# Setup of a fused attention and expert kernel: one activation table set, second-layer weights moved behind the first rows, one exp for both head parities of the last keys, one operation less in routing

## The chip, the cores and the metric

The kernel runs on one core of a Trainium2 chip. The metric is the time of one execution in microseconds (us) of device time. The engines are named as the profile names them: PE (matmuls; PEld is its weight load), DVE (vector), ACT (scalar, with function tables), POOL (general, here mostly the issuer of DMAs), SP (issuer of further DMAs). Each engine runs its own instructions in order and waits on the others by semaphores.

## The reference

Attention with a learned position bias (FIRE), then a mixture of eight experts in which every token has a given expert.

```python
# attention: batch 8, heads 8, seq 576, head_dim 64; hidden 32
scores = scale * q @ k^T
psi_rel = log1p(abs(i - j)); psi_i = log1p(max(i, 1))
x = (psi_rel / psi_i)[..., None]
bias = relu(x @ w1 + b1) @ w2            # one bias per (i, j, head), the same for all batches
attn = softmax(scores + bias)
x_rows = (attn @ v) as 4608 rows of 512  # batch and seq together, all heads side by side
# experts: 8 of them, 512 -> 1024 -> 512
out[rows of e] = relu(x_rows[rows of e] @ w1[e]) @ w2[e]
```

## The kernel before, in words

The program has three stages. **The bias stage** (the head of the program, up to about 56 us) computes exp(bias) once, for all heads, into fp16 tables that stay on chip: `biasM` for the keys 0 to 511, `biasR` for the last 64 keys, `biasL` and `biasRL` for the last 64 queries. **The attention stage** runs over eight batches; for each, 20 units of scores are made on PE, exponentiated on ACT (L585), multiplied by the tables on DVE (L596), and multiplied by v on PE (L609, L613). Its rows are scattered by POOL to DRAM (L673), sorted by expert. **The expert stage** (from about 226 us) reads them back transposed and runs the two matmuls of each expert on PE (L814, L790).

PE, DVE and ACT run their instructions in the order in which the program writes them (a manual schedule); POOL and SP are ordered by the framework's scheduler. The order around the change is as follows.

`_setup_constants` loads w1, b1 and w2 by three small DMAs on SP (L134, L136, L138), makes index ramps on POOL (L140 to L145), their logarithms on ACT (L158 to L165, L182, L183), and on DVE the slopes (L160 to L169), the negated b1 (`nb1`, L174) and `W2BIG` (L176, L178): a block-diagonal copy of w2, with four query rows times eight heads as its 32 columns. It is the second layer's weights. Then come, on DVE, the first operation of routing (L326) and three memsets of `_Attention.__init__` (L450, L452).

`_phase_bias` runs nine blocks `ib` of 64 queries (the ninth for the last 64). `hidden(ib)` makes 16 rows of hidden units, one per `k16`, each a tile of 128 (four queries times 32 units) by 576 keys: on ACT as a Relu with scale and bias (L220) for some `k16`, on DVE as multiply and max (L223) for the others. `outputs(ib)` takes the 16 rows through PE in three groups of keys: two groups of 2 x 128 keys (L240, 64 matmuls, 32 columns each) and the last 64 keys (L244, 16 matmuls with 64 stationary columns, into partitions 0 to 63 only). ACT exponentiates each group from PSUM: `biasM` in two operations (L256), and `biasR` in two operations of 64 partitions, one for the even and one for the odd heads (L253), each into its own half of the partitions. One raw part is copied by DVE (L260). The three groups share three PSUM buffers (`eb`). The program calls `hidden(ib + 1)` before `outputs(ib)`, so that the row work of a block stands ahead of the exponentials of the block before it. A row tile is used again two blocks later.

`_phase_route` is a generator: a chain of small DVE operations on 128x320 tables that gives each token its row in the sorted buffer; it is advanced by `next(route)` between the rows of the first blocks, and its rest (L352 to L408) runs on DVE at block 8, before the first attention units. Two of those operations are the overflow mask: `past = incl >= CAP` (L393) and `past = past * obase` (L395).

DMAs: POOL loads q, k and v of the first two batches and then weights, each issue waiting for an earlier one on its queue; SP copies the zeroed `vrag` tile to two others (L454) and fills the sorted buffer with zeros (L951), 9.25 MB.

Of the kernel before, what the change touches and what calls it, by code (L numbers as in the profile page):

```python
# [12 lines left out]
AO = mybir.AluOpType  # L13
AF = mybir.ActivationFunctionType
# [11 lines left out]
CAP = 640  # L26
# [11 lines left out]
NCOL = B * NT  # L38
# [36 lines left out]
def rap(t, off, dims, nparts=None):  # L75
    p0 = list(t.ap[0])
    if nparts is not None:
        p0[1] = nparts
    return bass.AP(tensor=t.tensor, offset=off, ap=[p0] + [list(d) for d in dims])
# [43 lines left out]
def _setup_constants(tc, G, w1, b1, w2):  # L123

    nc = tc.nc
    cst = G.cst
    w1col = cst.tile([P, 1], F32, tag="w1col", name="w1col")
    nc.sync.dma_start(out=w1col, in_=bass.AP(tensor=w1.tensor, offset=0, ap=[[0, 4], [1, 32], [1, 1]]))  # L134
    G.pb1 = cst.tile([P, 1], F32, tag="pb1", name="pb1")
    nc.sync.dma_start(out=G.pb1, in_=bass.AP(tensor=b1.tensor, offset=0, ap=[[0, 4], [1, 32], [1, 1]]))  # L136
    w2sb = cst.tile([HID, 8], F32, tag="w2sb", name="w2sb")
    nc.sync.dma_start(out=w2sb, in_=w2[:, :])  # L138
    li = G.tmp.tile([P, W4 + W1], I32, tag="li", name="li")
    nc.gpsimd.iota(li[:, 0:W4], base=-C4, channel_multiplier=0, pattern=[[1, W4]])  # L140
    si = G.tmp.tile([P, NGR], I32, tag="si", name="si")

    nc.gpsimd.iota(si[:, 0:128], base=0, channel_multiplier=0, pattern=[[1, 4], [16, 32]])
    nc.gpsimd.iota(si[:, 128:144], base=512, channel_multiplier=0, pattern=[[4, 16]])
    nc.gpsimd.iota(li[:, W4:], base=-(C1 + 512), channel_multiplier=0, pattern=[[1, W1]])  # L145

    gs = cst.tile([P, 5], F32, tag="gs", name="gs")
    nc.vector.memset(gs[:, 4:5], 1.0)
    for g in range(4):
        nc.vector.memset(gs[32 * g: 32 * g + 32, 0:1], float(g))  # L150
    for i, f in ((2, -4.0), (1, 4.0), (3, -1.0)):
        nc.vector.tensor_scalar(out=gs[:, i: i + 1], in0=gs[:, 0:1], scalar1=f, scalar2=None, op0=AO.mult)
    nc.vector.memset(G.zero[:, :, 0:DM], 0.0)
    lf = G.tmp.tile([P, W4 + W1], F32, tag="lf", name="lf")
    G.L4 = G.asb.tile([P, W4 + W1], F16, tag="L4", name="L4")
    G.slope = G.asb.tile([P, NGR], F32, tag="slope", name="slope")

    nc.scalar.activation(out=G.slope[:, 0:1], in_=gs[:, 4:5], func=AF.Ln, bias=1.0, scale=1.0)  # L158
    nc.scalar.activation(out=lf[:, 0:W4], in_=li[:, 0:W4], func=AF.Abs, bias=gs[:, 2:3], scale=1.0)
    nc.vector.tensor_scalar(out=G.slope[:, 0:128], in0=si[:, 0:128], scalar1=gs[:, 1:2], scalar2=1.0,  # L160
                            op0=AO.add, op1=AO.max)
    nc.vector.tensor_scalar(out=G.slope[:, 128:], in0=si[:, 128:], scalar1=gs[:, 0:1], scalar2=1.0,
                            op0=AO.add, op1=AO.max)
    nc.scalar.activation(out=G.slope, in_=G.slope, func=AF.Ln, bias=1.0, scale=1.0)
    nc.scalar.activation(out=G.L4[:, 0:W4], in_=lf[:, 0:W4], func=AF.Ln, bias=1.0, scale=1.0)  # L165

    def slopes(a, b):
        nc.vector.reciprocal(out=G.slope[:, a:b], in_=G.slope[:, a:b])
        nc.vector.tensor_scalar(out=G.slope[:, a:b], in0=G.slope[:, a:b], scalar1=w1col[:], scalar2=None,  # L169
                                op0=AO.mult)  # L170
    G.slopes = slopes
    slopes(0, 16)
    G.nb1 = cst.tile([P, 1], F32, tag="nb1", name="nb1")
    nc.vector.tensor_scalar(out=G.nb1, in0=G.pb1, scalar1=-1.0, scalar2=None, op0=AO.mult)  # L174
    G.W2BIG = G.asb.tile([P, 32], F16, tag="W2BIG", name="W2BIG")
    nc.vector.memset(G.W2BIG, 0.0)  # L176
    for g in range(4):
        nc.vector.tensor_scalar(  # L178
            out=G.W2BIG[32 * g: 32 * g + 32, 8 * g: 8 * g + 8],
            in0=w2sb, scalar1=8.0, scalar2=None, op0=AO.mult,  # L180
        )
    nc.scalar.activation(out=lf[:, W4:], in_=li[:, W4:], func=AF.Abs, bias=gs[:, 3:4], scale=1.0)  # L182
    nc.scalar.activation(out=G.L4[:, W4:], in_=lf[:, W4:], func=AF.Ln, bias=1.0, scale=1.0)  # L183
    G.idn = cst.tile([P, P], F16, tag="idn", name="idn")
    make_identity(nc, G.idn)


def _phase_bias(tc, G, route, at, fill):


    nc = tc.nc
    with tc.tile_pool(name="fps", bufs=1, space=bass.MemoryType.PSUM) as fps:
# [16 lines left out]
        def hidden(ib):  # L209
            hrl = []  # L210
            tiles = hidden_tiles(ib)
            for k16 in range(16):
                if ib < 8:
                    r, a = ib // 2, 16 * (ib % 2) + k16
                    m, c0 = 32 * r + a, C4 - (16 * a + r)
                else:
                    m, c0 = 128 + k16, W4 + C1 - 4 * k16
                hr = next(tiles)
                if k16 in ((2, 5, 8, 11, 14) if ib < 2 else (3, 8, 13)):
                    nc.scalar.activation(out=hr, in_=G.L4[:, c0: c0 + S], func=AF.Relu,  # L220
                                         bias=G.pb1[:], scale=G.slope[:, m: m + 1])
                else:
                    nc.vector.tensor_scalar(out=hr, in0=G.L4[:, c0: c0 + S],  # L223
                                            scalar1=G.slope[:, m: m + 1], scalar2=G.nb1[:],
                                            op0=AO.mult, op1=AO.max)
                hrl.append(hr)
                if (ib, k16) == (0, 7):
                    G.slopes(16, NGR)
                if (ib, k16) in ((1, 1), (1, 5), (1, 9), (2, 1), (2, 5)):
                    next(route)  # L230
            return hrl

        def outputs(ib, hrl):
            for jcs in ((0, 1), (2, 3), (4,)):
                eb = fps.tile([P, 2, 512], F32, tag="eb", name="eb", bufs=3)
                for k16 in range(16):
                    for lj, jc in enumerate(jcs):
                        hr = hrl[k16]
                        if jc < 4:
                            nc.tensor.matmul(out=eb[:, lj, 32 * k16: 32 * k16 + 32],  # L240
                                             lhsT=hr[:, jc: jc + 4 * 127 + 1: 4],
                                             rhs=G.W2BIG[:, 0:32], start=True, stop=True)
                        else:
                            nc.tensor.matmul(out=eb[0:64, lj, 32 * k16: 32 * k16 + 32],  # L244
                                             lhsT=hr[:, 512:576],
                                             rhs=G.W2BIG[:, 0:32], start=True, stop=True)
                ebv = eb.rearrange("p l (i h) -> p l h i", h=8)
                i0 = 64 * ib
                if jcs[0] == 4:
                    for h2 in range(2):  # L250
                        o = G.biasR[64 * h2: 64 * h2 + 64, :, i0: i0 + 64] if ib < 8 else \
                            G.biasRL[64 * h2: 64 * h2 + 64]
                        nc.scalar.activation(out=o, in_=ebv[0:64, 0, h2::2, :],  # L253
                                             func=AF.Exp, bias=0.0, scale=0.125)
                elif ib < 8:
                    nc.scalar.activation(out=G.biasM[:, jcs[0]: jcs[0] + 2, :, i0: i0 + 64], in_=ebv,  # L256
                                         func=AF.Exp, bias=0.0, scale=0.125)
# [3 lines left out]
                else:  # L261
                    for lj in range(2):
                        nc.scalar.activation(
                            out=G.biasL[:, jcs[0] // 2, lj, :, :, :].rearrange("p h q i -> p q h i"),
                            in_=ebv[:, lj, :, :].rearrange("p (q h) i -> p q h i", h=2),
                            func=AF.Exp, bias=0.0, scale=0.125)
# [36 lines left out]
def _phase_route(tc, G, dom2, x_dram):  # L303
# [7 lines left out]
    nc = tc.nc  # L311
# [10 lines left out]
    nc.gpsimd.memset(keep, 1.0)  # L322
    nc.gpsimd.memset(keep[:, :, 0:1], 0.0)
    nc.gpsimd.memset(keep[:, :, NCOL - NT: NCOL - NT + 1], 0.0)
    domf = pbuf.tile([P, NCOL], F32, tag="domf", name="domf")
    nc.vector.tensor_copy(out=domf, in_=dom2[:, :, :, 0].rearrange("p b t -> p (b t)"))  # L326
    yield
# [62 lines left out]
        nc.vector.tensor_tensor(out=v, in0=v, in1=rap(apref, i, [[2, 8], [0, c.stop - c.start]]), op=AO.add)  # L390
        yield
    past = pbuf.tile([P, 8, NCOL], F32, tag="past", name="past")
    nc.vector.tensor_scalar(out=past, in0=incl, scalar1=float(CAP), scalar2=None, op0=AO.is_ge)  # L393
    yield
    nc.vector.tensor_tensor(out=past, in0=past, in1=rap(obase, 0, [[1, 8], [0, NCOL]]), op=AO.mult)  # L395
    yield
    nc.vector.tensor_tensor(out=incl, in0=incl, in1=past, op=AO.add)
    yield
# [33 lines left out]
class _Attention:  # L432
# [10 lines left out]
    def __init__(self, tc, G, q, k, v, x_dram):  # L443
# [3 lines left out]
        nc, asb = self.nc, G.asb  # L447
        self.vrag = [asb.tile([P, 4, 130], F16, tag=f"vrag{i}", name=f"vrag{i}") for i in range(3)]

        nc.vector.memset(self.vrag[0], 0.0)  # L450
        for h2 in range(2):
            nc.vector.memset(self.vrag[0][64 * h2: 64 * h2 + 64, :, 65 * h2 + 64: 65 * h2 + 65], 1.0)  # L452
        for t in self.vrag[1:]:
            nc.sync.dma_start(out=t, in_=self.vrag[0])  # L454
        self.last = [asb.tile([P, 4, 2, 128], F16, tag=f"last{i}", name=f"last{i}") for i in range(2)]
# [550 lines left out]
```

## Time and profile before

| what | value |
|---|---|
| runs before | 375.62, 377.09, 372.06 and 410.43 us; median 376.36 |
| the profiled execution | 375.62 us, of which the span of the trace is 373.9 us (1.7 us lie around it) |
| busy in the span | PE 327.5 us, ACT 250.4, DVE 234.5, POOL 173.5 |
| mean granted PE clock | 0.949 |
| bias stage | 0 to about 56 us |
| attention stage | about 56 to 226 us |
| expert stage | about 226 to 368 us |

In the rows of the trace, the first two numbers are the start and the duration in us; then come the engine, the line, the operation, the tiles it writes and reads, their shape, and the count. Where one row stands for several instructions the duration is that from the start of the first to the end of the last. A bracket gives the idle time of the engine before the row, and what ended it. The duration of one instruction holds its latency; the pitch, from start to start, is what an engine spends on each.

### The profile page before, as it was taken

How to read it: one execution, taken by the hardware profiler on the slowest of the kernel's cores; microseconds unless marked ns; L12 is line 12 of the kernel's file. 1: busy time of each engine (PE TensorE's matmuls, PEld its weight loads, DVE VectorE, ACT ScalarE, POOL GpSimd, SP SyncE). 2: the span in 40 equal slices, each digit the busy share in tenths (PEclk: the TensorE clock that was granted, in tenths of full speed). 3: DMA queues.
4: the chain of work that ended last, by engine and by line, in shares of the span. 5: the costliest groups of instructions: out<-in, count | busy, mean ns of one | idle time of the engine just before them, and what ended most of it. 6: DMA issues, size and time to landing. Idle time of an engine off the chain costs nothing.

```text
span 373.9 us, 9668 instructions
## 1 busy us (share of the span) xinstructions
PE 327.5 (88%) x4098; PEld 213.4 (57%) x4098; DVE 234.5 (63%) x446; ACT 250.4 (67%) x306; POOL 173.5 (46%) x227
## 2 busy tenths in 40 slices
PE   1488696999898989898998779999999999999992
PEld 0387673667566656566574444565646565655551
DVE  6999999799999989898998673212030303021221
ACT  8999997799999989898999862341506051423330
POOL 9360101745949494958182605244534444441323
PEclk9999756799999999999998988999999999999997
DMA  5999999995898969496829742899999999930202
GB/s 88 182 154 353 366 326 232 161 197 84 120 181 115 189 111 185 89 187 114 124 69 175 168 65 69 158 232 206 190 187 230 150 216 235 260 153 28 110 28 101
DMA packets 87556, 61.58 MB, mean 165 GB/s; under 512 B 43605, under 2 KB 77653, under 8 KB 87512
## 3 DMA queue, kind: packets, MB, share of 16 engines
q0 software_dynamic: 55808, 45.12, 71.4%
q1 hardware_dynamic: 31704, 15.83, 19.5%
q8 instruction: 32, 0.52, 0.6%
q14 instruction: 12, 0.10, 0.1%
HBM read 61.93 MB, written 24.70 MB: 232 GB/s over the span
## 4 chain that ended last, share of the span: by engine, by line
DMA 17%; issue 14%; PE 10%; POOL 6%; ACT 4%; DVE 3%; POOLq 1%; DVEq 0%
DMA w<-in_moe_w_dram 12%; DMA out_dram<-res,ids 5%; POOL out_dram L794 5%; ACT e L585 4%; PE ops L790 2%; PE hps L824 2%; DVE e L596 2%; PE pu L613 1%; PE sc L559 1%; POOL w L758 1%; DVE xt L642 1%; PE pt L506 1%; PE pu L609 1%; PE sc L572 1%; PE hps L832 0%
## 5 line engine op out<-in xcount | busy, mean ns | idle before, releaser
L585 ACT ACTIVATE e<-sc 128x1024 f16<-128x1024 f32 x160 | 150.9, 1049 | 13.5 <-PE sc L559 6.1
L793 DVE COPY res<-ops 128x512 f32<-128x512 f32 x40 | 27.7, 692 | 111.3 <-PE ops L790 111.3
L852 ACT ACTIVATE hT<-hps 128x640 f16<-128x640 f32 x56 | 39.4, 704 | 77.4 <-PE hps L814 67.2
L596 DVE TENSOR_TENSOR e<-e,biasM 128x2048 f16<-128x2048 f16 x64 | 73.1, 1153 | 8.1 <-ACT e L585 5.7
L790 PE MATMUL ops<-w,hT 128*128 128x512 f16 x320 | 70.5, 379 | 0.0
L794 POOL DMA_INDIRECT out_dram<-res,ids x40 | 40.0, 999 | 65.4 <-DVE res L793 51.1
L673 POOL DMA_INDIRECT fire_x<-xt,posi x32 | 40.0, 1250 | 60.9 <-issue 42.9
L814 PE MATMUL hps<-xT,w 128*128 128x320 f16 x448 | 62.0, 299 | 0.3 <-PEq L869 0.3
L559 PE MATMUL sc<-qkT 64*128 64x512 f16 x256 | 51.9, 398 | 5.8 <-ACT e L585 4.0
L814 PEld LDWEIGHTS <-w 128*128 128x128 f16 x448 | 43.8, 98 | 18.7 <-issue 0.8
L790 PEld LDWEIGHTS <-hT 128*128 128x128 f16 x320 | 31.2, 98 | 36.5 <-ACT hT L826 0.3
L613 PE MATMUL pu<-vext,e 128*128 128x65 f16 x1024 | 51.0, 198 | 0.3 <-DVE e L596 0.3
L613 PEld LDWEIGHTS <-e 128*128 128x128 f16 x1024 | 45.2, 101 | 2.4 <-issue 1.1
L758 POOL DMA_DIRECT2D w<-in_moe_w_dram x32 | 25.2, 793 | 32.6 <-DMA w<-in_moe_w_dram 12.8
L240 PE MATMUL eb<-W2BIG,e 128*128 128x32 f16 x432 | 19.6, 193 | 16.5 <-DVE e L223 9.9
L609 PE MATMUL pu<-vrag,e 128*128 128x130 f16 x128 | 29.5, 230 | 3.0 <-DVE xt L642 1.1
L223 DVE TENSOR_SCALAR e<-L,slope,nb 128x576 f16<-128x576 f16 x86 | 30.8, 429 | 0.0
L240 PEld LDWEIGHTS <-e 128*128 128x128 f16 x432 | 17.4, 117 | 18.7 <-DVE e L223 10.9
L559 PEld LDWEIGHTS <-qkT 64*128 64x128 f16 x256 | 15.7, 93 | 21.0 <-issue 12.1
L609 PEld LDWEIGHTS <-e 128*128 128x128 f16 x128 | 12.7, 99 | 19.0 <-issue 10.8
L642 DVE TENSOR_TENSOR xt<-pu,rz 128x512 f16<-128x512 f32 (+1 forms) x33 | 22.3, 675 | 1.5
L531 DVE COPY qkT<-pt 128x1024 f16<-128x1024 f16 x32 | 21.9, 684 | 0.4 <-PE pt L506 0.3
(139 smaller groups left out, 384.0 us busy)
## 6 DMA issues: line engine op xcount, KB each, us to landing
w<-in_moe_w_dram POOLq DMA_DIRECT2D x32, 512.0 KB
fire_x<-zero SPq DMA_DIRECT2D x1, 5140.0 KB
fire_x<-zero SPq DMA_DIRECT2D x1, 4112.0 KB, 38.3
qn<-in_q_dram POOLq DMA_DIRECT2D x8, 512.0 KB
kn<-in_k_dram POOLq DMA_DIRECT2D x8, 512.0 KB
vst<-in_v_dram POOLq DMA_DIRECT2D x8, 512.0 KB
out_dram<-res,ids POOLq DMA_INDIRECT x40
last<-zero SPq DMA_DIRECT2D x2, 256.0 KB
```

Of the source, the lines that this page charges most:

```text
L223: nc.vector.tensor_scalar(out=hr, in0=G.L4[:, c0: c0 + S], scalar1=G.slope[:, m: m + 1], scalar2=G.nb1[:], op0=AO.mult, op1=AO.max)
L240: nc.tensor.matmul(out=eb[:, lj, 32 * k16: 32 * k16 + 32], lhsT=hr[:, jc: jc + 4 * 127 + 1: 4], rhs=G.W2BIG[:, 0:32], start=True, stop=True)
L559: mm(out=sc[:, h2, :], lhsT=self.qkT[b, p][hs[h2], 1, 128 * c: 128 * c + 128], rhs=self.qkT[b, p][hs[h2], 0, :], start=not raw, stop=True)
L585: nc.scalar.activation(out=ef[:, 0:n], in_=sf[:, 0:n], func=AF.Exp, bias=0.0, scale=0.125)
L596: self.nc.vector.tensor_tensor(out=job[0], in0=job[0], in1=job[1], op=AO.mult)
L609: mm(out=self.pu[:, c // 2, o: o + 130], lhsT=er[:, p % 2, 128 * c: 128 * c + 128], rhs=vr[:, p, :], start=True, stop=False, skip_group_ch ...
L613: mm(out=self.pu[:, c // 2, o + 65 * h2: o + 65 * h2 + 65], lhsT=self.e[b, ("m", p, j)][:, h2, 128 * c: 128 * c + 128], rhs=vx[:, 2 * p + ...
L673: inst = self.nc.gpsimd.indirect_dma_start(out=self.x_dram[:, :], out_offset=bass.IndirectOffsetOnAxis(ap=self.G.posi[0:n, c:c + 1], axis= ...
L790: nc.tensor.matmul(out=ops_, lhsT=hT[:, fc, t0: t0 + 128], rhs=G.w.w2(e, fc), start=(fc == 0), stop=(fc == 7))
L794: inst = nc.gpsimd.indirect_dma_start(out=out[:], out_offset=bass.IndirectOffsetOnAxis(ap=idx.bitcast(I32), axis=0), in_=res[:], in_offset ...
L814: nc.tensor.matmul(out=hps[:, i, 0:HC], lhsT=G.w.w1(e, dc)[:, 128 * fc: 128 * fc + 128], rhs=xT[:, dc, HC * hf: HC * hf + HC], start=(dc = ...
L852: nc.scalar.activation(out=hT[:, fc, :].rearrange("p (a b) -> p a b", a=2), in_=first(e, xT, ((fc, 0), (fc, 1))), func=AF.Relu, bias=0.0, ...
```

## The change

Six edits, all in the bias stage and its setup.

1. The table set `natural_log_exp_and_others` is loaded ahead of everything else on ACT, in place of two loads: one ahead of the first logarithm (L158) and one ahead of the first exp (L256).
2. The DMA of b1 is issued ahead of that of w1. `W2BIG` (L176, L178) and the first operation of routing (L326) are built behind the row `k16` = 6 of block 0, no longer ahead of all rows. On DVE that is behind five rows.
3. The memsets of `vrag` go from DVE to POOL.
4. The last 64 keys: each of the 16 matmuls is replaced by two of 16 columns each, even heads into partitions 0 to 63 and odd heads into 64 to 127. One exp over 128 partitions then takes the place of two over 64 (`biasR`, and `biasRL` in block 8).
5. In blocks 2, 3 and 4, four rows of 16 are made by ACT, where it was three.
6. The mask of routing is one operation in place of two.

The order of instructions on each engine follows from this: on ACT one table load and nine exps fewer, three rows more; on DVE three rows, three memsets and one routing operation fewer; on PE 144 matmuls more, each with its weight load. On POOL the memset of `vrag` stands ahead of the first load of q, its two small ones just behind that load.

```diff
+    nc.scalar.preload_act_table_set("natural_log_exp_and_others")
     w1col = cst.tile([P, 1], F32, tag="w1col", name="w1col")
-    nc.sync.dma_start(out=w1col, in_=bass.AP(tensor=w1.tensor, offset=0, ap=[[0, 4], [1, 32], [1, 1]]))
     G.pb1 = cst.tile([P, 1], F32, tag="pb1", name="pb1")
     nc.sync.dma_start(out=G.pb1, in_=bass.AP(tensor=b1.tensor, offset=0, ap=[[0, 4], [1, 32], [1, 1]]))
+    nc.sync.dma_start(out=w1col, in_=bass.AP(tensor=w1.tensor, offset=0, ap=[[0, 4], [1, 32], [1, 1]]))
...
-    nc.vector.memset(G.W2BIG, 0.0)
-    for g in range(4):
-        nc.vector.tensor_scalar(
-            out=G.W2BIG[32 * g: 32 * g + 32, 8 * g: 8 * g + 8],
-            in0=w2sb, scalar1=8.0, scalar2=None, op0=AO.mult,
-        )
+    def second_layer():
+        nc.vector.memset(G.W2BIG, 0.0)
...
+    G.second_layer = second_layer
...
-                if k16 in ((2, 5, 8, 11, 14) if ib < 2 else (3, 8, 13)):
+                if k16 in ((2, 5, 8, 11, 14) if ib < 2 else (2, 6, 10, 14) if ib < 5 else (3, 8, 13)):
...
+                if (ib, k16) == (0, 6):
+                    G.second_layer()
+                    next(route)
...
-                            nc.tensor.matmul(out=eb[0:64, lj, 32 * k16: 32 * k16 + 32],
-                                             lhsT=hr[:, 512:576],
-                                             rhs=G.W2BIG[:, 0:32], start=True, stop=True)
+                            for h2 in range(2):
+                                nc.tensor.matmul(out=eb[64 * h2: 64 * h2 + 64, lj, 16 * k16: 16 * k16 + 16],
+                                                 lhsT=hr[:, 512:576],
+                                                 rhs=G.W2BIG[:, h2::2], start=True, stop=True)
...
-                    for h2 in range(2):
-                        o = G.biasR[64 * h2: 64 * h2 + 64, :, i0: i0 + 64] if ib < 8 else \
-                            G.biasRL[64 * h2: 64 * h2 + 64]
-                        nc.scalar.activation(out=o, in_=ebv[0:64, 0, h2::2, :],
-                                             func=AF.Exp, bias=0.0, scale=0.125)
+                    nc.scalar.activation(out=G.biasR[:, :, i0: i0 + 64] if ib < 8 else G.biasRL,
+                                         in_=eb[:, 0, 0:256].rearrange("p (i q) -> p q i", q=4),
+                                         func=AF.Exp, bias=0.0, scale=0.125)
...
-    nc.vector.tensor_scalar(out=past, in0=incl, scalar1=float(CAP), scalar2=None, op0=AO.is_ge)
-    yield
-    nc.vector.tensor_tensor(out=past, in0=past, in1=rap(obase, 0, [[1, 8], [0, NCOL]]), op=AO.mult)
+    nc.vector.scalar_tensor_tensor(out=past, in0=incl, scalar=float(CAP), in1=rap(obase, 0, [[1, 8], [0, NCOL]]),
+                                   op0=AO.is_ge, op1=AO.mult)
...
-        nc.vector.memset(self.vrag[0], 0.0)
+        nc.gpsimd.memset(self.vrag[0], 0.0)
         for h2 in range(2):
-            nc.vector.memset(self.vrag[0][64 * h2: 64 * h2 + 64, :, 65 * h2 + 64: 65 * h2 + 65], 1.0)
+            nc.gpsimd.memset(self.vrag[0][64 * h2: 64 * h2 + 64, :, 65 * h2 + 64: 65 * h2 + 65], 1.0)
```

More of the change, by code (lines that the diff above doesn't have):

```diff
@@ L175, in _setup_constants @@
     G.W2BIG = G.asb.tile([P, 32], F16, tag="W2BIG", name="W2BIG")
-    nc.vector.memset(G.W2BIG, 0.0)
-    for g in range(4):
-        nc.vector.tensor_scalar(
-            out=G.W2BIG[32 * g: 32 * g + 32, 8 * g: 8 * g + 8],
-            in0=w2sb, scalar1=8.0, scalar2=None, op0=AO.mult,
-        )
+    def second_layer():
+        nc.vector.memset(G.W2BIG, 0.0)
+        for g in range(4):
+            nc.vector.tensor_scalar(
+                out=G.W2BIG[32 * g: 32 * g + 32, 8 * g: 8 * g + 8],
+                in0=w2sb, scalar1=8.0, scalar2=None, op0=AO.mult,
+            )
+    G.second_layer = second_layer
     nc.scalar.activation(out=lf[:, W4:], in_=li[:, W4:], func=AF.Abs, bias=gs[:, 3:4], scale=1.0)
@@ L324, in _phase_route @@
     nc.gpsimd.memset(keep[:, :, NCOL - NT: NCOL - NT + 1], 0.0)
+    yield
     domf = pbuf.tile([P, NCOL], F32, tag="domf", name="domf")
```

## The prediction

> **What bounds the kernel now.** I read the stretches first, to see which stage passes a gain on (columns: stretch, length, busy us and count of PE, PEld, DVE, ACT, POOL, then clock, DMA share, GB/s).
>
> ```profile
> 16.00:30.00 14.00, 10.17 (x237) 9.66 (x237) 13.42 (x43) 13.88 (x21) 8.66 (x12) 1.00 1.40 179
> 41.00:56.00 15.00, 12.05 (x258) 10.78 (x257) 14.59 (x47) 14.35 (x24) 0.89 (x1) 0.54 1.10 343
> 56.00:76.00 20.00, 17.18 (x229) 11.00 (x229) 17.46 (x31) 15.52 (x18) 8.12 (x13) 0.75 1.20 198
> 226.00:340.00 114.00, 114.00 (x699) 66.20 (x696) 23.01 (x38) 37.68 (x52) 48.40 (x53) 0.99 1.02 187
> ```
>
> The expert stage is PE without a gap and is not edited, so it keeps its length; a gain must come from the first 60 us and be carried through 170 us of attention. In the bias stage ACT (13.88 of 14) and DVE (13.42 of 14) are both nearly full, PE is not. That is the central point: work taken off one of them alone shows only until the other is the bound. The chain of waits gives nothing here, its listed pieces begin at 162 us. So I read the head in order of time, first ACT:
>
> ```profile
> 14.81 1.28 ACT L256 ACT_TABLE_LOAD   x1
> 16.10 1.94 ACT L256 ACTIVATE biasM<-eb 128x1024 f16<-128x1024 f32 x2
> ...
> 28.47 2.39 ACT L220 ACTIVATE e<-L,pb,slope 128x576 f16<-128x576 f16 x3
> 30.77 1.91 ACT L256 ACTIVATE biasM<-eb 128x1024 f16<-128x1024 f32 x2
> 32.58 0.75 ACT L253 ACTIVATE biasR<-eb 64x256 f16<-64x256 f32 x2
> 33.36 0.87 ACT L220 ACTIVATE e<-L,pb,slope 128x576 f16<-128x576 f16 x1
> ```
>
> From starts: three rows 2.30 (0.766 each), biasM 1.81, biasR 0.78: a block is 4.89 on ACT. The last biasRL ends at 56.2. DVE:
>
> ```profile
> 5.56 1.08 DVE L178 TENSOR_SCALAR W2BIG<-w2sb 32x8 f16<-32x8 f32 x4 [0.17 <-DMA w2sb<-in_w_dram]
> 6.84 0.28 DVE L450 MEMSET vrag<- 128x260 uint32 x1
> 7.40 2.27 DVE L223 TENSOR_SCALAR e<-L,slope,nb 128x576 f16<-128x576 f16 x6
> ...
> 18.07 0.29 DVE L260 CAST biasW<-eb 128x128 f16<-128x128 f32 x1 [0.58 <-ACT biasM L256]
> ...
> 56.72 0.33 DVE L393 TENSOR_SCALAR past<-incl 128x320 f32<-128x320 f32 x1
> ```
>
> Thirteen rows (28.12 to 32.71) are 4.6, so 0.35 a row, and a block with its cast is 4.7 to 4.8. After block 8, DVE runs the rest of routing until 59.88, and in the first batch ACT waits on it and PE (PE stood 2.00 us on the qkT copy behind routing). So DVE's end of the head sets the start of the attention. Last PE, for the last-key matmuls:
>
> ```profile
> 34.17 1.04 PE L244 MATMUL eb<-W2BIG,e 128*64 128x32 f16 x16
> 35.14 1.03 PE L506 MATMUL ptl<-idn,last 128*128 128x128 f16 x8
> ...
> 79.88 0.22 PE L624 MATMUL pu<-vrag,e 128*64 128x65 f16 x2
> 79.94 0.30 PE L628 MATMUL pu<-vext,e 128*64 128x65 f16 x8
> 80.07 0.20 PE L624 MATMUL pu<-vrag,e 128*64 128x65 f16 x2
> 80.65 0.62 PE L506 MATMUL ptl<-idn,last 128*128 128x128 f16 x8
> ```
>
> The same eight transposes took 1.03 at 35.14 and 0.62 at 80.65, so PE was slow in the bias stage already, though the granted clock reads 1.00 until 40 us.
>
> **The change part by part.**
>
> *Table load.* One of two loads goes: 1.28 on ACT, on the path, since the next ACTIVATE starts at 16.10, just at its end. The first load stays where it is (0.97, first on ACT in both orders). [...]
>
> *DVE before the first rows.* The w1 DMA, now second on SP, lands when b1 did, at about 5.2; so L169 starts there and not at 4.09, takes 0.3, nb1 0.1, and rows start at 5.65. Five rows 1.8, W2BIG 1.2 and L326 0.2, one row, slopes 1.2: the slopes end at 10.4, before at 10.85. So 0.45 is gained: the vrag memsets (0.56) and the 0.17 wait, less 0.3 for w1. That the weights stand behind rows gives nothing by itself; the same work is only permuted. PE starts at about 8.6 and not at 7.88, and costs nothing, as it then idled 1.20 for rows. ACT waited 0.86 for these slopes, so its block-1 rows also start 0.45 sooner.
>
> *POOL and SP.* The vrag memset lies between the 0.35 of a 128x320 fp32 memset and nothing, the two small ones at 0.15 each (a 128x8 one). The first q load starts some 0.5 later, k and v some 0.8. SP's vrag copy waits for the small memsets, at about 6.5, where it started at 7.39. Behind it POOL waited 5.88 for the copy, so the loads behind that are 0 to 0.9 sooner. q and k are first read at 36, and v after the routing: covered by over 10 us. Without that cover it would cost 0.8. The fill (23.42) waits for a DVE memset and moves with it.
>
> *Exps of last keys.* Nine times two 64x256 exps (0.39 each from starts) become one of 128x256; the row for that shape is scx, 0.396 in duration against 0.373, so 0.39. ACT gains 9 x 0.39 = 3.5.
>
> *Three rows to ACT.* ACT 3 x 0.766 = 2.3 dearer, DVE 3 x 0.35 = 1.05 cheaper.
>
> *Mask.* L393 goes, 0.36 from its start to that of L395 (57.08), if the fused operation costs L395's 0.49; between 0.4 gained and 0.1 lost.
>
> *Last-key matmuls.* Now 32 a block in place of 16. L244 cost 0.06 each (0.97 from 34.17 to 35.14), all in one half of the array. Alternating halves have two rows: L624 and L628, ten from 79.88 to 80.07, 0.019 each at full clock; and the pt transposes (L506), eight from 36.10 to 36.53 at the slow clock, 0.054 each for 128 columns. I take 0.038, twice 0.019 for the clock: 1.22 a block against 0.97. Ends: 0.019 (0.61) and 0.06 (1.92). [...] PE has room: 64 matmuls at 0.036 are 2.3, plus 1.22 makes 3.5 of a block's 4.5 to 5.3.
>
> *The sum.* Per block, ACT and DVE now cost: blocks 2 to 4, ACT 4 x 0.766 + 1.81 + 0.39 = 5.26 and DVE 12 x 0.35 + 0.2 = 4.4; later, ACT 4.50 and DVE 4.75. The larger one counts: 3 x 5.26 + 4 x 4.75 = 34.8, before 7 x 4.89 = 34.2. ACT's own total falls by 1.28 + 0.45 + 3.5 - 2.3 = 2.9, but ACT is the bound in three blocks and DVE in the others. Stepping through: biasM of block 0 starts at 14.3 (16.10), then 19.6, 24.8, 30.1 (21.00, 25.88, 30.77). DVE's cast of block 3, which waits for biasM, comes at 32.0 (32.71), and from there DVE needs what it did. So DVE is 0.7 sooner at the end of the blocks, plus 0.36 in routing: 1.1. Carried through: 375.6 - 1.1 = **374.5 us**. The median is 0.7 above the profiled run and holds the 410; I stay with the profiled run. For the clock I add 3 us on either side: runs 372.06 to 377.09 already differ by 5.
>
> **The rivals.**
>
> *All of ACT's gain arrives:* 2.9, if DVE rows run nearer 0.34 (as in the 23.50 to 27.92 group) and ACT's exps pace the first batch: 372.7. For: ACT idled only 0.5 us in the blocks. Against: DVE's routing stands before the first batch.
>
> *The clock:* PE granted 0.54 and 0.75 from 41 to 76. From its first scores (L565, 55.35) to those of the next batch (79.36) the first batch took 24.0, the next, from scx exp to scx exp (75.94, 95.69), 19.75; ACT idled 4.5 of the 20 us. If PE stays at full clock there, up to 4.2 more: 370.3, and 368 with all of ACT's gain. For: PE gets more work in its gaps. Against: PE is idle 1.5 for biasM in each block, as before.
>
> *Slower, by the last-key matmuls:* at 0.06 each PE pays 0.96 more at the end of block 8, where the first scores stand behind them, and 0.5 around the transposes of block 5, in place of the gain: about 376.5 to 377. PE becomes the bound of the blocks beyond 0.075 each (2.3 + 32x = 4.7). For 2% slower (7.5, with the 1.1 back) nine blocks must each run over by about 0.96: 0.105 each, about 383. Against: the 0.019 and 0.054 rows.
>
> *Nothing arrives:* the lead goes into waits at 196 to 216 us (POOL's issue waited 9.06, weights landing over 12.28): 375.6. Against: these loads are issued by the progress of attention.
>
> **How the numbers follow.** Forecast 0.50, all of ACT's 0.17, the clock 0.12, last-key matmuls 0.13, nothing 0.08. A difference within 2% is about what a measurement of this kernel can tell from no change. Its edges are 368.1 and 383.1. Faster than that takes the clock case in full and some of another: 0.11. Slower takes the matmuls far beyond their rows, or a worse clock: 0.10. Same: 0.79. The likeliest case's own range is 371.5 to 377.5; with the others 368 to 380.5.
>
> **What would show it.** One table load, near 1 us; biasM of block 0 near 14.3; biasR alone near 0.39; last-key matmuls, from start to start, near 0.04; the first rows near 5.65; the cast of block 3 near 32.0; routing's end near 58.8. The expert stage as long as before. The forecast is wrong if PE stands without gaps in the blocks, if the batch after the head is longer or shorter by more than 2 us, or if the w1 DMA lands late.

## The result, and the profile after

The ratio of the changed kernel to the one before is 0.9883, with a 95% interval of 0.9825 to 0.9941: about 4.4 us less, within the 2% that counts as no difference here. The medians do not show it (375.98 us of 12 runs, 375.62 of 17 before), because five runs of 12 after and six of 17 before took 389 to 416 us, and the ratio leaves out every run more than 1.5% above the fastest of its kernel (after, those of 374.09 and 377.87 too). The runs left range from 366.4 to 371.4 us after, and from 372.0 to 377.1 before.

The profiled execution after took 377.87 us (span 376.2). It carries a DMA that comes late in the expert stage, which the last of these rows of PE shows:

```profile
222.32 7.07 PE L829 MATMUL hps<-xA,w 128*128 128x512 f16 x32
...
314.74 11.14 PE L819 MATMUL hps<-xT,w 128*128 128x320 f16 x64 [5.62 <-DMA xT<-fire_x]
```

The same group takes 8.86 elsewhere, so 5.62 + 2.28 of this run do not belong to the kernel; without them it is 370.0. In every profile without such a wait, and with the first expert matmuls at 7.07, the span ends 145.8 to 146.0 us after the first expert matmul. So the expert stage is as long as it was, and the start of that matmul, plus 145.9, plus the 1.7 around the span, tells what a run would take: 369.9 here. Everything below is therefore told from the first 222 us. (Line numbers are up to 7 higher than before.)

The stretches of the changed kernel, in the columns of before:

```profile
16.00:30.00 14.00, 10.13 (x290) 9.80 (x290) 13.93 (x44) 14.00 (x20) 7.21 (x10) 1.00 1.46 222
41.00:56.00 15.00, 13.70 (x286) 10.93 (x287) 14.69 (x49) 11.71 (x19) 0.00 (x0) 1.00 1.09 328
56.00:76.00 20.00, 17.77 (x256) 11.72 (x257) 17.85 (x28) 16.24 (x19) 9.26 (x15) 1.00 1.12 182
```

In the early blocks ACT and DVE are both full, as before. In the late ones ACT has room (11.71 of 15, before 14.35) and DVE has not: DVE is the bound there. ACT in order of time:

```profile
0.97 1.28 ACT L133 ACT_TABLE_LOAD   x1 [0.97 <-PEq L995]
...
10.99 1.63 ACT L223 ACTIVATE e<-L,pb,slope 128x576 f16<-128x576 f16 x2 [0.97 <-DVE slope L169]
...
14.80 1.91 ACT L261 ACTIVATE biasM<-eb 128x1024 f16<-128x1024 f32 x2
...
44.97 0.44 ACT L257 ACTIVATE biasR<-eb 128x256 f16<-128x256 f32 x1
45.24 2.46 ACT L223 ACTIVATE e<-L,pb,slope 128x576 f16<-128x576 f16 x3
```

One load is left, ahead of everything. biasM of block 0 starts at 14.80 (before 16.10). ACT waited 0.97 for the slopes, a little more than the 0.86 of before. One biasR exp takes 0.27 from its start to the next instruction's. DVE:

```profile
5.28 0.23 DVE L169 TENSOR_SCALAR slope<-slope,w1col 128x16 f32<-128x16 f32 x1 [1.24 <-DMA w1col<-in_w_dram]
5.43 0.14 DVE L174 TENSOR_SCALAR nb<-pb 128x1 f32<-128x1 f32 x1
5.68 2.22 DVE L226 TENSOR_SCALAR e<-L,slope,nb 128x576 f16<-128x576 f16 x5
...
9.15 0.63 DVE L226 TENSOR_SCALAR e<-L,slope,nb 128x576 f16<-128x576 f16 x1
...
10.67 0.29 DVE L169 TENSOR_SCALAR slope<-slope,w1col 128x128 f32<-128x128 f32 x1
...
32.10 0.29 DVE L265 CAST biasW<-eb 128x128 f16<-128x128 f32 x1 [0.73 <-ACT biasM L261]
...
55.85 0.49 DVE L399 SCALAR_TENSOR_TENSOR past<-incl,obase 128x320 f32<-128x320 f32 x1
...
58.47 0.18 DVE L413 CAST posi<-posf 128x40 int32<-128x40 f32 x1
```

The rows start at 5.68, but the slopes still end at 10.96 (10.85 before). At block 3 DVE waits 0.73 for ACT, so ACT sets the early blocks. The mask is one operation of 0.49. Routing ends at 58.65 (59.88 before). PE:

```profile
33.51 1.02 PE L251 MATMUL eb<-W2BIG,e 128*64 128x16 f16 x32
34.46 1.03 PE L511 MATMUL ptl<-idn,last 128*128 128x128 f16 x8
...
60.51 0.64 PE L511 MATMUL pt<-idn,qn 128*64 128x128 f16 x8 [1.49 <-DVE qkTl L536]
...
65.73 0.64 PE L511 MATMUL pt<-idn,kn 128*64 128x128 f16 x8
...
69.51 0.41 PE L511 MATMUL pt<-idn,qn 128*64 128x128 f16 x8
```

The 32 last-key matmuls of a block take 0.95 from 33.51 to 34.46, 0.030 each; 16 of the old kind took 0.97. I read the clock from the eight transposes `pt`: low where they take 0.64, up to 65.7 at least, and full where they take 0.41, at 69.5, though the granted clock of the page reads 1.00 at both. (In the kernel before they took 0.64 at 64.36, at a granted 0.50, and 0.41 at 61.74, at 1.00.)

### The profile page after: what moved, and what is told of

The parts are those of the page before. It is cut to its first block, busy times and chain, and to the rows that moved or that the text cites. A ratio compares the mean times of both kernels' runs of the same rounds, so it can differ in the third digit from the quotient of the medians.

```text
span 376.2 us, 9946 instructions
## 1 busy us (share of the span) xinstructions
PE 326.4 (87%) x4242; PEld 212.2 (56%) x4242; DVE 232.7 (62%) x439; ACT 246.8 (66%) x299; POOL 176.7 (47%) x230
## 4 chain that ended last, share of the span: by engine, by line
issue 16%; DMA 15%; PE 11%; ACT 7%; POOL 5%; DVE 2%; POOLq 1%; DVEq 0%
DMA w<-in_moe_w_dram 9%; ACT e L590 7%; DMA out_dram<-res,ids 6%; POOL out_dram L799 4%; PE ops L795 2%; PE hps L829 2%; PE sc L564 2%; PE pu L618 1%; DVE e L601 1%; PE sc L577 1%; POOL w L763 1%; PE pt L511 1%; PE pu L614 1%; DVE xt L647 0%; PE hps L837 0%
## 5 line engine op out<-in xcount | busy, mean ns | idle before, releaser
L819 PE MATMUL hps<-xT,w 128*128 128x320 f16 x448 | 64.3, 306 | 5.9 <-DMA xT<-fire_x 5.6
L618 PE MATMUL pu<-vext,e 128*128 128x65 f16 x1024 | 48.9, 194 | 0.3 <-DVE e L601 0.3
L618 PEld LDWEIGHTS <-e 128*128 128x128 f16 x1024 | 43.1, 98 | 2.2 <-issue 0.8
L614 PE MATMUL pu<-vrag,e 128*128 128x130 f16 x128 | 28.7, 224 | 3.4 <-DVE xl L665 1.5
L246 PEld LDWEIGHTS <-e 128*128 128x128 f16 x432 | 17.2, 117 | 17.0 <-DVE e L226 9.7
L614 PEld LDWEIGHTS <-e 128*128 128x128 f16 x128 | 12.4, 97 | 18.5 <-issue 9.5
```

Source lines behind the costliest of these rows:

```text
L246: nc.tensor.matmul(out=eb[:, lj, 32 * k16: 32 * k16 + 32], lhsT=hr[:, jc: jc + 4 * 127 + 1: 4], rhs=G.W2BIG[:, 0:32], start=True, stop=True)
L614: mm(out=self.pu[:, c // 2, o: o + 130], lhsT=er[:, p % 2, 128 * c: 128 * c + 128], rhs=vr[:, p, :], start=True, stop=False, skip_group_ch ...
L618: mm(out=self.pu[:, c // 2, o + 65 * h2: o + 65 * h2 + 65], lhsT=self.e[b, ("m", p, j)][:, h2, 128 * c: 128 * c + 128], rhs=vx[:, 2 * p + ...
L819: nc.tensor.matmul(out=hps[:, i, 0:HC], lhsT=G.w.w1(e, dc)[:, 128 * fc: 128 * fc + 128], rhs=xT[:, dc, HC * hf: HC * hf + HC], start=(dc = ...
```

## Experiments

The theory: in each block the larger of ACT and DVE counts, and DVE's end of the head (the end of routing, L413) sets what follows. The rivals: ACT's whole gain arrives; or the time comes from PE's clock at the start of the attention and not from the head. The runs were made on three chips, each beside runs of the kernel before on the same chip, to which its ratio is taken.

**Both kernels again.** No edit.

> The kernel before, unchanged, for a second profile. Theory head (the change saves about 1.1 us up to the end of routing and nothing else; the rest of the 4.4 us is what the clock of PE did in the last batch): routing ends again at 59.9, the first last-batch scores come again near 199, but the expert stage starts anywhere from 222 to 227, and the low-clock stretches of 200 to 226 need not come back. Rival (the rest comes from the change): the expert stage starts again within 0.5 us of 226.4, with the clock near 0.87 from 200 to 226.

> The changed kernel, unchanged, for a second profile and more times. Theory head: routing ends at 58.65 again, the expert stage starts between 221 and 226, and the 5.6 us wait for a transpose in the expert stage does not come back. Rival: the expert stage starts within 0.5 us of 222.3. The ratio to the kernel before should lie between 0.982 and 0.994 by the times so far.

The four profiles, in us from the span's start; the first batch is from routing's end to its `scx` exp, the last stage from the `scx` exp of batch 6 to the first expert matmul:

| profile | routing's end | first batch | last stage | first expert matmul |
|---|---|---|---|---|
| before | 59.88 | 16.06 | 31.16 | 226.37 |
| before, again | 59.92 | 15.99 | 29.42 | 224.39 |
| after | 58.65 | 15.80 | 28.50 | 222.32 |
| after, again | 58.40 | 14.02 | 28.50 | 220.66 |

The head is 1.2 to 1.5 shorter. What comes behind it differs between two profiles of the same program: by 1.7 in the last stage before, by 1.8 in the first batch after. The first expert matmul at 220.66 lies just below the 221 to 226 that was expected. The rule of 145.9 + 1.7 gives 368.3 for the second profile after; it took 368.18. In that profile PE has its full clock just behind routing and has no gap there (compare 60.51 above):

```profile
47.95 0.49 PE L246 MATMUL eb<-W2BIG,e 128*128 128x32 f16 x10 [1.44 <-issue]
...
54.42 0.55 PE L246 MATMUL eb<-W2BIG,e 128*128 128x32 f16 x12 [1.56 <-issue]
...
60.40 0.54 PE L511 MATMUL pt<-idn,qn 128*64 128x128 f16 x8
60.78 0.39 PE L511 MATMUL pt<-idn,kn 128*64 128x128 f16 x8
```

Its PE also stands 1.44 and 1.56 us in the blocks, waiting for nothing that the profile shows. We come back to that.

**Three rows of 16 on ACT in all blocks from 2** (edit 5 undone).

```diff
-                if k16 in ((2, 5, 8, 11, 14) if ib < 2 else (2, 6, 10, 14) if ib < 5 else (3, 8, 13)):
+                if k16 in ((2, 5, 8, 11, 14) if ib < 2 else (3, 8, 13)):
```

> The changed kernel with three ACT rows, not four, in blocks 2, 3 and 4. Theory that the larger of ACT and DVE counts in each block: ACT 0.76 a block less and no longer the bound there, DVE 3 x 0.35 more; DVE loses its 0.73 wait at the cast of block 3, so routing ends 0.3 us later (59.0), and the time is within 0.3 us of the changed kernel's. Rival that ACT's total counts: routing's end and the time 2.3 us sooner.

Routing ended at 58.88, ratio 0.9982 (0.9940 to 1.0024). DVE does not wait for biasM at all and is the bound throughout. The two shares of rows are within 0.2 to 0.5 of each other (58.65 and 58.40 with the edit), as the larger of two says: what ACT gave up, DVE had to do.

**One matmul and two exps for the last keys, as before** (edit 4 undone).

```diff
-                            for h2 in range(2):
-                                nc.tensor.matmul(out=eb[64 * h2: 64 * h2 + 64, lj, 16 * k16: 16 * k16 + 16],
+                            nc.tensor.matmul(out=eb[0:64, lj, 32 * k16: 32 * k16 + 32],
...
```

> The changed kernel with the last keys as before: 16 matmuls, two exps of 64 partitions. Theory that the larger counts: ACT costs 0.5 a block more, 5.6 in blocks 2 to 4 and 4.9 later, and DVE waits for it: routing ends 2 to 3 us later (60.7 to 61.5), later than in the kernel before, and the time is 2 to 3 us longer than the changed kernel's. PE's last-key work per block stays near 1.0 us. Rival that DVE alone sets the end: routing ends at most 0.5 us later.

Routing ended at 60.50, ratio 1.0008 (0.9978 to 1.0037). The blocks are 5.64 with four ACT rows and 4.88 with three, 0.53 more than with the edit, and DVE waits 2.3 for biasM. With the four rows in, edit 4 carries 1.85 to 2.1, and without it the head is 0.6 longer than before.

**Edit 4 alone, in the kernel before.**

> The kernel before with the edit of the last keys alone. Theory that the larger of ACT and DVE counts: ACT falls to 4.5 a block, DVE stays at 4.75, only DVE's small waits go: routing ends 0.3 to 0.6 us sooner (59.3 to 59.6) and the time is about 0.5 us shorter. Rival that ACT's total counts: 2 to 3.5 us shorter.

Routing ended at 59.56, 0.3 sooner than before; blocks of 4.35 to 4.6 on ACT, and DVE the bound. No ratio came of its four runs. ACT's 9 x 0.5 us saved are worth 0.3 as long as DVE keeps its rows.

**Two table loads, as before** (edit 1 undone: the preload's line left out).

> The changed kernel with two table loads, as before. Theory: biasM of block 0 starts at 16.1 and not 14.8, ACT is the bound in blocks 2 to 4, so the 1.28 stays: routing ends at 59.6 to 59.9, and the time is 1.0 to 1.3 us longer than the changed kernel's. Rival (DVE sets the end, and ACT has room): routing ends within 0.4 us of 58.6.

biasM of block 0 at 16.21, routing's end at 59.81, so the load is worth 1.16 to 1.4 there, nearly its 1.28. Ratio 1.0009 (0.9928 to 1.0090).

**Second-layer weights in front of the rows, w1 ahead of b1** (edit 2 undone).

> The changed kernel with edit 2 undone: w1 ahead of b1 on SP, the second-layer weights and the first operation of routing ahead of all rows. The slopes ended at 10.96 with edit 2 and at 10.85 before, so theory (edit 2 moves work about and gives nothing): slopes end at 10.7 to 11.0, biasM of block 0 starts at 14.6 to 15.0 (14.80 in the changed kernel), routing ends at 58.4 to 58.9 (58.65), time as the changed kernel's. Rival (the edit saves its 1.25 of weights and routing in front of the first rows): PE's first matmuls or the rows come later by that, biasM of block 0 at 15.5 or later, routing's end at 59.3 or later. A third: without the wait for w1 the slopes end 0.4 sooner, at 10.5, and biasM of block 0 starts at 14.3.

The third reading came nearest (the slopes end at 10.60, expected 10.5). DVE at its start, and the end of routing:

```profile
4.08 1.22 DVE L169 TENSOR_SCALAR slope<-slope,w1col 128x16 f32<-128x16 f32 x1
5.23 0.15 DVE L174 TENSOR_SCALAR nb<-pb 128x1 f32<-128x1 f32 x1
...
6.83 2.58 DVE L226 TENSOR_SCALAR e<-L,slope,nb 128x576 f16<-128x576 f16 x6
9.34 0.94 DVE L168 RECIPROCAL slope<-slope 128x128 f32<-128x128 f32 x1
10.31 0.29 DVE L169 TENSOR_SCALAR slope<-slope,w1col 128x128 f32<-128x128 f32 x1
...
57.99 0.18 DVE L409 CAST posi<-posf 128x40 int32<-128x40 f32 x1
```

The next row starts at 10.51, 0.36 sooner than with the edit (10.87): nb1 starts at 5.23 and not at 5.43, and the six rows take 2.51, from 6.83 to 9.34, where in the changed kernel five took 2.17 and the one behind the weights 0.55. biasM of block 0 starts at 14.44, routing ends at 58.17. So edit 2 costs 0.36 in the chain to biasM and 0.2 to 0.5 at routing's end. By time it can't be told from the changed kernel (368.6, 368.9, 371.7 us; ratio 0.9944, 0.9882 to 1.0005).

**ACT's rows shared out otherwise**: 36 in all, where the changed kernel has 34 (the count in the expectation is wrong).

```diff
-                if k16 in ((2, 5, 8, 11, 14) if ib < 2 else (2, 6, 10, 14) if ib < 5 else (3, 8, 13)):
+                if k16 in ((2, 5, 8, 11, 14) if ib in (0, 1, 8) else (2, 6, 10, 14) if ib in (2, 4, 6) else (3, 8, 13)):
```

> The changed kernel with ACT's rows shared out otherwise: five in blocks 0, 1 and 8, four in 2, 4 and 6, three in 3, 5 and 7, so 34 in place of 35... the last two being in block 8, where ACT waited 2.73 us for PE ahead of biasL. DVE has as many rows less in block 8 as the two that ACT takes (0.35 each). Theory (the larger of ACT and DVE counts in each block, DVE's end of the head decides): DVE's routing ends 0.3 to 0.7 sooner, at 58.0 to 58.4, first expert matmul sooner by as much. Rival (at the end of the blocks PE is what counts, since the rows of block 8 are followed by its 64 matmuls in 3.9): routing's end and the first scores stay within 0.2 of the changed kernel's.

Routing ended at 57.68, 0.7 to 1.0 sooner, more than expected: 0.7 for two rows of 0.35, and at most part of the 0.73 wait at block 3, since no two blocks of four ACT rows follow each other (DVE waits 0.2 for biasM in all). Its time gained nothing (370.1 and 373.1 us, ratio 0.9993, 0.9919 to 1.0067): in its profile the first batch took 16.04, the last stage 31.05, and the first expert matmuls took 8.96 for 7.07 (before 8.76, at a mean granted clock of 0.81 up to 235.4).

**Filler matmuls, in the kernel before and in the changed one.** 128x128 matmuls that nothing reads: 16 at each of five places of the last batch; 24, 8 and 8 in the first three gaps of the first batch; both, in the changed kernel.

```diff
+            if (b, ui) in ((0, 2), (0, 3), (0, 4)):
+                self.spin(24 if ui == 2 else 8, self.G.aps, "pu", 1)
...
+                elif what[0] == "T" and b == B - 1:
+                    self.spin(16, self.G.tps, "tr", 2)
```

> The kernel before, with 16 matmuls without a use at each of the five places of the last batch where other batches have their transposes. Theory clock (part of the 4.4 us is that PE ran at low clock in stretches of the last batch before, 31.2 and 29.4 us from the last key exp of batch 6 to the first expert matmul, against 28.5 in four profiles of changed kernels): that stretch is 28.5 to 29, and the time 0.5 to 2.5 us shorter than before. Rival (the dips are chance, and idle of DVE and ACT, not PE's clock, sets the stretch): 29.4 or more, and the time the same or longer.

> The kernel before, with 24, 8 and 8 matmuls without a use ahead of the transposes of the first batch's units 2, 3 and 4, where PE waits 2 us and goes back to the low clock. Theory clock (one profile of the changed kernel had PE at full speed from 61 and its first batch was 2.0 us shorter than in the other): the transposes after 62 take 0.41 for eight and not 0.64, the last key exp of batch 0 starts near 74 and not at 75.9, and the time is 1.5 to 2 us shorter. Rival (DVE's chain sets the first batch): the exp stays at 75.5 to 76.5.

> The changed kernel with filler matmuls that nothing reads: 24 + 8 + 8 of 128x128 in the first three gaps of PE in the first batch, and 16 in the last batch's tail. Clock theory (the part of the gain that the head does not give comes where PE's gaps at the start of the first batch do not let its clock fall; fillers made that batch 13.76 in place of 15.99 in the kernel before, and the last stage 28.34 in place of 29.42): first batch, from routing's end to the scx exp, 13.7 to 14.1; last stage, scx exp of batch 6 to the first expert matmul, 28.3 to 28.6; first expert matmul at 220.3 to 220.9; time of most undisturbed runs 367 to 369, 1.5 to 2.5% below before. Rival (the fillers only cost PE time; the two durations of the first batch are drawn anew in each run): first batch 15.5 to 16 in the profile, time 370 to 372 as the median of the changed kernel's runs.

In the kernel before, the last stage was 28.34 with the fillers at the end, and the first batch 13.76 with those at the start, as the clock theory says. But the last stage of that second run, which has no fillers there, was 28.49, so the first run does not show that fillers shorten it. The time followed in the second case only, and not clear of noise (369.87 and 369.90 us, ratio 0.9936, 0.9864 to 1.0008; at the end 1.0007, 0.9950 to 1.0063). In the changed kernel both together gave a last stage of 28.31, but a first batch of 15.26, though the granted clock was 1.00 from 59.6 us on: 24 fillers took 2.10, most of it at the low clock, to 60.4, and used up the lead of the head. So a full clock there is not enough by itself. The two fastest runs with both took 370.8 and 371.4: no gain. The gap of PE behind routing and the spells of granted clock 0.5 stand together:

| profile | PE's wait for DVE there | clock 0.5 after 59 us | first batch |
|---|---|---|---|
| before, again | 2.22 | 62.3 to 69.1 | 15.99 |
| edit 4 alone | 1.84 | 62.1 to 68.9 | 16.03 |
| rows otherwise | 1.93 | 60.3 to 67.1 | 16.04 |
| edit 2 undone | 0.97 | 62.3 to 65.7 | 15.06 |
| edit 1 undone | 0.99 | to 61.0 only | 13.75 |
| before, fillers | filled | none | 13.76 |
| after, both fillers | filled | to 59.6 only | 15.26 |

Behind the waits of 1.84 to 2.22 the low clock came back, for 6.8 us; with a wait of just under 1 it came back for 3.4 in one profile and not in the other; with the gap filled it did not. How a wait would bring it back, no run shows.

**Each last-key matmul issued twice**: 64 a block in place of 32, the same output.

```diff
-                            for h2 in range(2):
+                            for h2 in (0, 1, 0, 1):
```

> The changed kernel with each last-key matmul issued twice (64 a block in place of 32; same output). In the changed kernel 32 of them took 0.95 a block (33.51 to 34.46), 0.030 each. Theory (PE has the room, DVE and ACT pace the blocks): a block gains 0.95 on PE, 4.2 of 4.35, hidden beside biasM; biasM to biasM stays at 5.11 and 4.35 to 4.5; only the end of block 8 shows it, so the first scores come up to 0.95 later, but routing's end stays at 58.6 to 58.9 and the first expert matmul moves by 0 to 0.5. Rival of the prediction (matmuls of 16 columns at 0.06 each, PE becomes the bound): 1.9 more a block, biasM to biasM at 5.3 or more in blocks 5 to 8, routing's end later by 2 or more, time 2 to 8 us longer.

The theory fell. Ratio 1.0188 (1.0144 to 1.0232); biasM to biasM 5.1 to 7.1, on average (56.65 - 14.80) / 7 = 5.98; first scores 10.9 later and the first expert matmul 8.5. But the rival's reason fell too, for the matmuls cost what was expected, 64 in 1.8:

```profile
52.28 1.77 PE L251 MATMUL eb<-W2BIG,e 128*64 128x16 f16 x60 [2.67 <-issue]
...
58.75 0.81 PE L251 MATMUL eb<-W2BIG,e 128*64 128x16 f16 x24 [2.26 <-issue]
...
63.53 1.88 PE L251 MATMUL eb<-W2BIG,e 128*64 128x16 f16 x64
```

The waits from 16 us to the end of the blocks (who waited, for whom, us in all, times, longest), PE's and then ACT's:

```profile
PE eb L251 <- issue: 11.6, 6, 2.7
```

```profile
ACT biasR L257 <- PE eb L251: 9.6, 6, 2.4
```

PE stood 11.6 us in six waits behind no engine and no data. They end at 26.75, 33.49, 39.96, 46.09, 52.28 and 58.75, in front of PE's matmuls number 351, 479, 607, 734, 862 and 990 (counted from 0): one every 128. The DMA queue that the profile calls "instruction" has the same period, and nothing else was found that has it (packets, MB, share of the DMA engines):

```profile
q8 instruction: 36, 0.59, 0.6%
```

Its packets are of 16384 bytes, and there are 32 in the kernel before, 33 in the changed one and 36 here. In this run they start at 24.3, 30.9, 37.5, 43.8, 50.1 and 56.4 and take 0.9 to 1.1 each; every wait ends 2.2 to 2.6 after one starts. Before, 4098 matmuls and as many weight loads are 32.0 times 256, and the changed kernel's 4242 are 33.1 times: as if each packet held 256 of PE's instructions, which would be 64 bytes each, an estimate from these counts and the packets' size. From 25 to 57 us, where the DMA engines move 308 to 334 GB/s on average in each profile, most of it SP's fill, no profile has two of these packets less than 5.9 us apart, and most are 6 to 7 apart. The next two here, at 60.5 and 64.1, came 4.1 and 3.6 apart, the first of them while the engines still moved 360 GB/s. So it is not shown that the fill holds these packets up; no run left it out.

So in this stage PE met a limit besides its own: from the end of one wait to the end of the next, 128 matmuls took 6.1 to 6.7 us here, about 0.05 each, where 64 without a wait took 0.034 each at 32 columns (from 61.35 to 63.53) and 0.028 at 16 (to 65.33). That the wait is for PE's instructions is read from the common period. Before, 80 matmuls in a block of 4.89 (7.8 for 128) stood clear of that figure. The changed kernel has 96 in 4.35 to 5.11 (5.8 to 6.8 for 128): at its edge. Its second profile stands 3.0 us at numbers 734 and 862, and three other kernels with its matmul count (edit 4 alone, edit 1 undone, edit 2 undone) 0.8 to 1.0 at the same numbers; the first profile does not. These waits cost nothing seen. The first scores came at 55.85 in place of 54.40, about as much later as PE had waited for DVE behind routing in the first profile (1.49). They may even be why that gap was gone and PE had its full clock there in the second profile; this was not tried.

## Why the prediction was right, and where its steps were not

Predicted 374.5, from 375.6 and a gain of 1.1 in the head. The head gave 1.2 to 1.5. The ratio gives 4.4, which puts 375.6 at 371.2: inside the range with the rivals (368 to 380.5) and just under the likeliest case's own (371.5 to 377.5). The sign and the class hold, and the step that the forecast rests on is shown; the other 3 us are not in the forecast's sum, though the clock rival left room for them, so that the class held is not all the forecast's merit.

*The larger of ACT and DVE* was the right step: undoing edit 5 moved routing by 0.2 to 0.5, edit 4 alone gave 0.3 of its 4.5, and ACT's 2.9 did not arrive in the head. Edit 5 needs edit 4: without edit 4 the head was longer than before (60.50), and beside it edit 5 is worth 0.2 to 0.5.

*The table load* (1.28) came as a start of biasM 1.30 sooner, and 1.16 to 1.4 by its undo.

*The slopes* were the step that failed. "So 0.45 is gained": they ended 0.11 later than before. The first rows started at 5.68 as said (5.65), but five of them took 2.17 in place of 1.8, and the one behind the weights 0.55 in place of 0.35. The pitch of 0.35 had been taken from rows at 28 us. The undo shows that the edit costs 0.36 there. The excess lies in single rows, and it comes beside POOL's issuing of loads:

```profile
5.68 0.62 DVE L226 TENSOR_SCALAR e<-L,slope,nb 128x576 f16<-128x576 f16 x1
6.22 0.41 DVE L226 TENSOR_SCALAR e<-L,slope,nb 128x576 f16<-128x576 f16 x1
6.44 1.01 POOL L481 DMA_DIRECT2D kn<-in_k_dram  x1
...
6.90 0.67 DVE L226 TENSOR_SCALAR e<-L,slope,nb 128x576 f16<-128x576 f16 x1
```

In the fourteen profiles 87 of DVE's rows in the bias stage took more than 0.5 us, and every one of them ran beside a DMA issue of POOL; of the 1065 rows that did not, none took so long. (Another 404 beside such an issue stayed under 0.5.) Why one row in several is held up there was not tried.

*The exp of 128x256* was put at 0.39 and spends 0.27: a duration had been taken where a pitch was needed. So the blocks were 5.11 and 4.35 (predicted 5.26 and 4.50). This made up for the slopes: from 14.80, 0.5 later than said, three blocks of 5.11 lead to 30.12, where 30.1 had been said, and the cast of block 3 came at 32.10 (32.0). Two wrong terms of one size met in a right sum.

*The last-key matmuls* took 0.030 each, where 0.038 was said: a pair costs no more than the 0.061 of one of the old form. But "PE becomes the bound of the blocks beyond 0.075 each" sets the wrong limit. It counted matmul time only; the doubled run reached the bound at 0.030.

*The mask* gained 0.36 as said. The memsets moved to POOL delayed the first load of q from 4.57 to 5.11, and nothing waited for it.

*The clock* was the rival nearest to the rest. Of the 4.4, 1.2 to 1.5 is the head. The two profiles with a low clock in the first batch, before (again) and after, are 2.07 apart at the first expert matmul, 1.27 from the head and most of the rest from the last stage (29.42 and 28.50). Up to 1.8 more appears when PE has its full clock in the first batch, as in the second profile after; there the batch was 2.04 shorter than before (14.02 and 16.06), just past the 2 us that the prediction named as a sign of being wrong. One profile with fillers supports this for the first batch of the kernel before; that the change makes the full clock more frequent is not shown. Undoing edit 5 moved the head by 0.2 to 0.5 and the ratio from 0.988 to 0.998, and two kernels with heads 0.5 and 1.0 shorter than in the changed kernel's first profile were not timed faster: some 3 us are decided behind the head, and how much of them belongs to the change stays open. None of the versions run beats the changed kernel.

## What to carry to other kernels

When two engines are both nearly full, a saving on one shows only until the other is the bound: alone, edit 4 gave 0.3 of its 4.5. Moving work between them is worth trying then, but count it: it added 0.2 to 0.5 here. Sum an engine's chain from pitches and not from durations (0.27 against 0.44 for one exp). Before adding many small instructions to an engine, count them too: here, with each last-key matmul issued twice, 128 of PE's matmuls took 6.1 to 6.7 us from one wait without a seen cause to the next, though 64 of 16 columns took but 1.8, and the ratio was 1.0188.

## What the hardware showed that was not expected

PE's waits, read as waits for its own instructions, 0.3 to 2.7 us each, 128 matmuls apart. Two matmuls of 16 columns into alternate halves of the output's partitions cost 0.059 together, no more than one of 32 columns into one half (0.061). Rows on DVE took 0.62 and 0.67 in place of 0.41 beside POOL's issuing of loads. And waits of PE of 1.84 to 2.22 us were followed by 6.8 us at a granted clock of 0.5, while the granted clock of the page reads 1.00 in stretches where the same transposes take 0.64 and not 0.41.
